# Dummy matmuls only behind the first list, K's first parts from ScalarE's queue, VE's copies on GpSimd, a shorter first list, more slack for the routing

## The chip, the cores and the metric

The kernel runs on one core of a Trainium2 chip. That core has TensorE (PE, matrix products), VectorE (DVE), ScalarE (ACT), GpSimd (POOL) and SyncE (SP), and 16 DMA engines that move data between the device's memory and the core. DMAs are issued from queues of SP, ACT and POOL. The metric is the device time in microseconds (us); the lower, the better.

## The reference

Two stages follow each other: windowed attention over 8 batches of 8 heads, 576 positions and 64 dimensions, and a layer of 8 experts over the 4608 resulting tokens.

```python
scores = scale * np.matmul(q, k.transpose(0, 1, 3, 2))      # [8, 8, 576, 576]
mask = (rel >= 0) & (rel < 64)                              # each row sees 64 positions
attn = softmax(np.where(mask, scores, -1e9))                # over the last axis, + 1e-9
x = np.matmul(attn, v) -> [4608, 512]                       # heads side by side

logits = x @ w_gate                                         # [4608, 8]
for idx in np.argsort(-logits.flatten()):                   # best pair first
    tok, e = idx // 8, idx % 8
    if assigned[tok] >= 0 or counts[e] >= 576: continue
    assigned[tok] = e; counts[e] += 1
for e in range(8):
    mask = assigned == e
    out[mask] = np.maximum(x[mask] @ w1[e], 0) @ w2[e]      # 512 -> 1024 -> 512
```

Each expert so ends with exactly 576 tokens, and which ones is known only when all gates are known and a round of counting is done for the experts in turn.

## The kernel before, in words

**Attention** (`attention`) goes in 72 steps, each for two blocks of 64 positions and four of the eight heads. A step is a short pipeline over PE, DVE and ACT: QK products into a PSUM tile Sp (L126), masked softmax on DVE (L135), exponentials on ACT (L145), transposes on PE (L152), products with the values into Op (L173), and the normalisation into x (L198), which DVE does four steps later. Q, K, VT (the values transposed, for the gates) and VO (the values as they are, with the gate columns beside them) come per batch through SP's queue; batches 0 and 1 come in parts, batch 2 and those behind it whole, and load_all(b) is issued in step 9(b-2)+5. The two loads of K's first part stand on GpSimd's queue. VO has three buffers, VE two. VE is VO shifted by 64 rows, so that windows of the other parity find their rows on the same partitions: `even` makes it by two copies for each tile of positions (L111, L112), on DVE for some tiles and on GpSimd for others. Ahead of `even` the gates of a batch go through PE (gate_mm, L85), ACT (gate_cp), PE (gate_tr, L95) and DVE (gate_out, L101), which writes them into VO.

At the end of attention, when fewer than four steps are in flight, each step also issues five matmuls on a tile of zeros (L274), whose result nobody reads: dummies.

**Routing** (`Routing.steps(p)`) makes expert p's list. Eight rounds narrow down the threshold of the expert whose turn it is: compare on DVE, count by 36 products on PE (L523 for p = 0, L537 for p above), pr on DVE (L569), a product num (L572), a new threshold. Then the list follows: code, eid, q and the marks X on DVE (L616 to L630), a scan, positions by PE (L647, L648), a one-hot product (L687) and the indices idx (L696, L701). The update of eid and of the counts (L708 to L729, with the product cn at L724) is made behind idx. For the first list nothing else is there to do, and the list stands on the path. `warm(n)` issues n dummies (L473); it is called four times a round, after pos, behind the list with 28, and in `turn`.

**Experts** (`Experts`) take three streams each. `load` brings weights: a part `st` by DMA, wh on ACT (L800, fp32 rounded down), -wh into wl on ACT (L809), and an accumulating DMA from GpSimd (L811) that adds st to wl, the low part. Parts 0 to 2 of expert 0 make wl on DVE instead. `turn` gathers the tokens with five indirect DMAs on GpSimd (L853), transposes them on PE (L865), and evacuates them as xh on ACT (L842) and xl on DVE (L845), for five tiles of 128 tokens (the last of 64). `steps` makes the products: 12 matmuls in three groups, wh xh, wl xh, wh xl, into h (L909), hh on ACT (L883) and hl on DVE (L888); then the second products (L941 for the last 64 tokens, L951 for the others), and out through ACT (L923, L926) and an indirect DMA (L931).

**What sets the order.** Attention's order is written out by hand. Behind it a planner, `Streams`, runs routing, loads, turns and products as generators, each yielding an estimate of the time until its next step (`slack` is added to some of these, by SLACK[p]) or a condition; the order in which it takes them is the order of instructions on each engine. A change of one estimate so moves instructions on every engine. The products of expert p start when its XT is set, each unit when its weights stand in W and `tiles` covers its columns.

## Time and profile before

| | us |
|---|---|
| median of 3 runs | 678.64 |
| lowest and highest | 677.87, 678.86 |
| the profiled execution | 681.14 |
| its span in the trace | 679.50 |
| outside the span | 1.64 |
| PE busy | 651.4 (96%) |
| DVE busy | 451.8 (66%) |
| ACT busy | 360.9 (53%) |
| POOL busy | 177.5 (26%) |

The profile is of one execution. The first row of its second part gives PE's busy share in 40 slices of 17 us: it is 9 nearly everywhere, 6 and 8 in the first two, and 8 and 7 in slices 11 and 12, where attention has ended and the first list is made. The row below it on the clock has 6 and 7 there. Busy matmuls are counted whether they are of use or dummies, and a busy PE at a lower clock gets less done, so the busy share must be read with the granted clock (1.00 is 2.4 GHz, 0.50 is 1.2 GHz).

### The profile page before, as it was taken

Reading aid. Unit: us, or ns where it says so; the run is one execution under the profiler, and the core shown is the slowest. Engines: PE = TensorE matmul, PEld = TensorE weight load, DVE = VectorE, ACT = ScalarE, POOL = GpSimd, SP = SyncE. Lnnn points to the kernel's source line nnn. Section 1 sums busy time; section 2 is a strip of 40 time slices with the busy share of each in tenths; the row PEclk is TensorE's granted clock in tenths of the full one; section 3 lists DMA queues with packets and bytes.
Section 4 is the critical chain, followed back from the end, with each engine's and each line's share of the span. In section 5 each row is a group of like instructions: output and inputs, shape, how many; then the busy total and the mean of one; then the engine's idle time right before and its main releaser. Section 6 shows DMA issues by size and latency. Waiting matters only on the chain. (4 is left out here: it accounts for less than half of the span.)

```text
span 679.5 us, 17084 instructions
## 1 busy us (share of the span) xinstructions
PE 651.4 (96%) x6451; PEld 544.1 (80%) x6451; DVE 451.8 (66%) x2262; ACT 360.9 (53%) x733; POOL 177.5 (26%) x203
## 2 busy tenths in 40 slices
PE   6899999999879989999999999999999999999995
PEld 5577777777559868897898799789889889989984
DVE  4989999988677766896896787787777611320300
ACT  4678888886034517617447166355616715634410
POOL 1321222220032116206125133322412443112011
PEclk9899999999679989999999999999999999999998
DMA  8999988922046539849779767939938994952501
GB/s 280 329 357 364 363 309 306 389 96 79 17 143 187 114 75 314 198 80 306 191 143 288 191 147 249 224 82 267 219 101 169 295 273 103 252 150 77 95 23 47
DMA packets 49683, 134.11 MB, mean 197 GB/s; under 512 B 4672, under 2 KB 10432, under 8 KB 49600
## 3 DMA queue, kind: packets, MB, share of 16 engines
q0 software_dynamic: 15552, 54.01, 35.3%
q1 hardware_dynamic: 34048, 79.00, 32.9%
q8 instruction: 51, 0.84, 0.5%
q14 instruction: 32, 0.26, 0.1%
HBM read 82.13 MB, written 18.87 MB: 149 GB/s over the span
## 5 line engine op out<-in xcount | busy, mean ns | idle before, releaser
L888 DVE SCALAR_TENSOR_TENSOR hl<-h,hh 128x256 fp32r<-128x256 f32 x128 | 53.5, 418 | 95.2 <-ACT hh L883 94.5
L951 PE MATMUL o<-wh,hl 128*128 128x512 f32 x256 | 102.1, 399 | 0.0
L951 PE MATMUL o<-wh,hh 128*128 128x512 f32 x256 | 102.1, 399 | 0.0
L951 PE MATMUL o<-wl,hh 128*128 128x512 f32 x256 | 101.3, 396 | 0.0
L145 ACT ACTIVATE pe<-st,mx 128x128 f32<-128x128 f32 x288 | 91.3, 391 | 8.6 <-DVE mx L135 7.2
L883 ACT ACTIVATE hh<-h 128x256 fp32r<-128x256 f32 (+1 forms) x128 | 52.1, 407 | 79.0 <-PE h L909 77.6
L909 PE MATMUL h<-xh,wh 128*128 128x256 f32 (+1 forms) x512 | 93.8, 301 | 0.0
L909 PE MATMUL h<-xh,wl 128*128 128x256 f32 (+1 forms) x512 | 92.0, 298 | 0.0
L909 PE MATMUL h<-xl,wh 128*128 128x256 f32 (+1 forms) x512 | 92.0, 298 | 0.0
L135 DVE CUSTOM_DVE_ANT_0 st<-Sp,mask 128x128 f32<-128x128 f32 x288 | 78.6, 277 | 17.9 <-PE Sp L126 13.4
L931 POOL DMA_INDIRECT out<-ot,idx x40 | 40.2, 1005 | 190.6 <-ACT ot L923 61.6
L923 ACT ACTIVATE ot<-o 128x512 f32<-128x512 f32 x32 | 19.1, 597 | 120.0 <-PE o L951 120.0
L909 PEld LDWEIGHTS h<-xh,wh 128*128 128x128 f32 x512 | 76.6, 190 | 1.4 <-issue 0.7
L909 PEld LDWEIGHTS h<-xh,wl 128*128 128x128 f32 x512 | 75.8, 190 | 0.3
L909 PEld LDWEIGHTS h<-xl,wh 128*128 128x128 f32 x512 | 75.8, 190 | 0.1
L811 POOL DMA_DIRECT2D wl<-st x61 | 55.1, 1065 | 74.7 <-ACT wl L809 58.7
L800 ACT ACTIVATE wh<-st 128x1024 fp32r<-128x1024 f32 x64 | 67.3, 1052 | 12.4 <-DMA st<-w 12.3
L853 POOL DMA_INDIRECT xg<-xs,idx x40 | 42.2, 1054 | 114.9 <-DVE eq L708 62.0
L809 ACT ACTIVATE wl<-wh 128x1024 fp32r<-128x1024 f32 x61 | 64.4, 1056 | 0.4
L951 PEld LDWEIGHTS o<-wl,hh 128*128 128x128 f32 x256 | 48.4, 189 | 9.2
L951 PEld LDWEIGHTS o<-wh,hl 128*128 128x128 f32 x256 | 48.3, 189 | 9.2
L951 PEld LDWEIGHTS o<-wh,hh 128*128 128x128 f32 x256 | 48.4, 189 | 8.9
(177 smaller groups left out, 1164.4 us busy)
## 6 DMA issues: line engine op xcount, KB each, us to landing
wl<-st POOLq DMA_DIRECT2D x61, 512.0 KB, 7.1
st<-w SPq DMA_DIRECT2D x59, 512.0 KB, 7.3
xs<-x SPq DMA_DIRECT2D x36, 256.0 KB, 4.9
VO<-v SPq DMA_DIRECT2D x6, 1168.0 KB, 16.8
VT<-vt SPq DMA_DIRECT2D x6, 1152.0 KB, 11.4
Q<-q SPq DMA_DIRECT2D x6, 1152.0 KB, 13.9
K<-k SPq DMA_DIRECT2D x6, 1152.0 KB, 15.4
st<-w POOLq DMA_DIRECT2D x5, 512.0 KB, 6.0
```

What stands on the lines that cost most here:

```text
L135: nc.vector.tensor_tensor_reduce(st[:, h, :], Sp[h % 2][:, h // 2], mk, scale=-0.125, scalar=3.0e38, op0=OP.add, op1=OP.min, accum_out=mx[ ...
L145: nc.scalar.activation(pe[:, h, :], st[:, h, :], AF.Exp, bias=mx[:, h:h + 1], scale=-1.0)
L800: nc.scalar.activation(hi, st[i], AF.Copy)
L809: nc.scalar.activation(lo, hi.bitcast(FT), AF.Copy, scale=-1.0)
L811: nc.gpsimd.dma_start(lo.bitcast(FT), st[i], accum_op=OP.add)
L853: nc.gpsimd.indirect_dma_start(out=g[0:n, a], out_offset=None, in_=self.xs, in_offset=IndirectOffsetOnAxis(ap=idx[0:n, a:a + 1], axis=0))
L883: nc.scalar.activation(hh[:, f, c0:c1], h, AF.Relu)
L888: nc.vector.scalar_tensor_tensor(t, h[:, a - c0:b - c0], 0.0, hh[:, f, a:b].bitcast(FT), op0=OP.max, op1=OP.subtract)
L909: nc.tensor.matmul(h, wv[:, cc, 128 * (f % 2):128 * (f % 2) + 128], xt[:, cc, c0:c1], start=(k == 0), stop=(k == 11))
L923: nc.scalar.activation(ot, o, AF.Copy)
L931: nc.gpsimd.indirect_dma_start(out=self.out, out_offset=IndirectOffsetOnAxis(ap=idx[0:m, a:a + 1], axis=0), in_=ot[0:m], in_offset=None)
L951: nc.tensor.matmul(o, ht[:, f, 128 * a:128 * a + 128], wt[:, 512 * (f % 2):512 * (f % 2) + 512], start=(k == 0), stop=(k == 23))
```

## The change

K's two loads of the first part of batch 0 are issued from ACT's queue instead of POOL's. `even` runs on DVE for batch 0's first two tiles alone, and on GpSimd for all others; eight pairs of copies move. The dummies of attention's last steps, those of the rounds, the ten after pos and the second six in the first turn go away; 28 behind the list and six in the turn stay. For the first list the operation on eid moves behind idx, and X is made from q directly. XT is set at the start of a turn; a unit of products waits for `tiles`, which counts xh alone, and its third group for `lows`, which counts xl. SLACK is 100 for all experts but the first, and the product cn of experts 2 and up has 1500 ahead of it.

```diff
--- before.py
+++ after.py
@@ -208,8 +208,8 @@
             if b or i[0]:
                 load_qk(b, *i)
             else:
-                load_qk(b, *i, slice(0, 2), nc.gpsimd)
-                load_qk(b, *i, slice(2, 4), nc.gpsimd)
+                load_qk(b, *i, slice(0, 2), nc.scalar)
+                load_qk(b, *i, slice(2, 4), nc.scalar)
                 nc.sync.dma_start(wgbd, wg)
                 counters()
             load_vt(b, *i)
@@ -236,7 +236,7 @@
             put(s + 1, gate_out, b, *i)
             for j in range(4):
                 if i[0] <= 2 * j + 2 < i[1]:
-                    put(s + 1, even, b, j, nc.vector if 4 * b + j <= 2 or (b, j) == (1, 0) or b > 1 and not j else nc.gpsimd)
+                    put(s + 1, even, b, j, nc.gpsimd if b or j > 1 else nc.vector)
     for b in range(2, B):
         put(9 * (b - 2) + 5, load_all, b)
     last = []
@@ -268,11 +268,6 @@
             pv(*seq[s - 3])
         for f, a in at.get(s, []):
             f(*a)
-        if s >= n:
-
-            for _ in range(5):
-                nc.tensor.matmul(SP[0][0].rearrange("p h w -> p (h w)"), z, z[:, None, :].to_broadcast([128, 2, 128]),
-                                 start=True, stop=True)
         if late:
             late.pop(0)()
         if s > 3:
@@ -346,7 +341,7 @@
 NR = 8
 FAR = 2.0 ** 101
 OWN = 2
-SLACK = (0, 0, 0, 0, 100, 100, 100, 100)
+SLACK = (0,) + (100,) * 7
 U32 = mybir.dt.uint32
 
 
@@ -570,8 +565,6 @@
                     yield self.dve(220) + slack
                     num = self.room(128, E, not p)
                     nc.tensor.matmul(num, self.ones[0:ND], pr, start=True, stop=True)
-                    if not p:
-                        self.warm(4)
                     yield self.busy(110) + 200 + slack
                 thr2 = tile_([128, ND], I32, name="thr")
                 if r == 0:
@@ -617,17 +610,20 @@
                                            accum_out=code)
 
             eid = self.eid
-            ab = tile_([128, NJ], FT, name="ab") if p else eid
-            nc.vector.scalar_tensor_tensor(ab, m, T[:, 0:1], best, op0=OP.is_gt, op1=OP.mult)
             self.expert(p, code)
-            yield self.dve(600)
             q = tile_([128, NJ], FT, name="q")
             nc.vector.tensor_scalar(q, best, code, None, op0=OP.is_equal)
+
+            nc.vector.scalar_tensor_tensor(X[:, 1], m, T[:, 0:1], q, op0=OP.is_equal, op1=OP.mult)
+            yield self.dve(600)
             if p:
+                ab = tile_([128, NJ], FT, name="ab")
+                nc.vector.scalar_tensor_tensor(ab, m, T[:, 0:1], best, op0=OP.is_gt, op1=OP.mult)
                 nc.vector.tensor_tensor(eid, eid, ab, OP.add)
-
-            nc.vector.scalar_tensor_tensor(X[:, 1], m, T[:, 0:1], q, op0=OP.is_equal, op1=OP.mult)
-            nc.vector.tensor_scalar(X[:, 0], eid, code, None, op0=OP.is_equal)
+                nc.vector.tensor_scalar(X[:, 0], eid, code, None, op0=OP.is_equal)
+            else:
+
+                nc.vector.scalar_tensor_tensor(X[:, 0], m, T[:, 0:1], q, op0=OP.is_gt, op1=OP.mult)
             yield self.dve(600)
         else:
             pr8 = tile_([128, E], FT, name="pr8")
@@ -646,8 +642,6 @@
         pos = self.room(128, 2 * NJ, not p)
         nc.tensor.matmul(pos, self.tri, Xf, start=True, stop=False)
         nc.tensor.matmul(pos, self.ones, run, start=False, stop=True)
-        if p == 0:
-            self.warm(10)
         yield self.busy(150) + 200 + slack
         Y = tile_([128, 2, NJ], FT, name="Y")
         nc.vector.scalar_tensor_tensor(Y.rearrange("p k j -> p (k j)"), pos, 1.0, Xf,
@@ -704,6 +698,8 @@
         if p < E - 1:
             if p == 0:
                 yield 3000
+            if not p:
+                nc.vector.scalar_tensor_tensor(self.eid, m, T[:, 0:1], best, op0=OP.is_gt, op1=OP.mult)
             eq = tile_([128, NJ], FT, name="eq")
             nc.vector.scalar_tensor_tensor(eq, Y[:, 1], CAP + 0.5, X[:, 1], op0=OP.is_lt, op1=OP.mult)
             nc.vector.scalar_tensor_tensor(self.eid, eq, code[:, 0:1], self.eid, op0=OP.mult, op1=OP.add)
@@ -719,7 +715,7 @@
             c2 = tile_([128, E], BF, name="c2")
             with nc.allow_low_precision(reason="whole numbers up to 36"):
                 nc.vector.tensor_reduce(c2, self.oh.rearrange("p j e -> p e j"), axis=AX.X, op=OP.add)
-            yield self.dve(900) + slack
+            yield self.dve(900) + (slack if p < OWN else 1500)
             cn = self.room(128, E)
             nc.tensor.matmul(cn, self.ones, c2, start=True, stop=True)
             yield self.busy(110) + 200 + slack
@@ -764,6 +760,7 @@
         self.sent = 0
         self.turned = 0
         self.tiles = [0] * E
+        self.lows = [0] * E
 
     def room(self):
         return self.ps.tile([128, 320], FT, name="h", bufs=3)
@@ -840,12 +837,11 @@
             r = slice(128 * a, 128 * a + n)
             t = t.bitcast(FT)
             nc.scalar.activation(xh[:, :, r], t[:, :, :n], AF.Copy)
+            self.tiles[p] = a + 1
             yield 700
             self.busy(600, "dve")
             nc.vector.tensor_tensor(xl[:, :, r], t[:, :, :n], xh[:, :, r].bitcast(FT), OP.subtract)
-            self.tiles[p] = a + 1
-            if a == 1:
-                self.XT[p] = (xh, xl)
+            self.lows[p] = a + 1
 
         g = fw.tile([128, 5, DM], FT, name="xg")
         for a in range(5):
@@ -857,6 +853,7 @@
         yield lambda: self.first == p
         xh = fw.tile([128, NX, CAP], FR, name="xh")
         xl = fw.tile([128, NX, CAP], FR, name="xl")
+        self.XT[p] = (xh, xl)
         for a in range(5):
             n = 128 if a < 4 else 64
             yield max(0, there - 1280 * (4 - a) - self.clock())
@@ -865,7 +862,7 @@
                 nc.tensor.transpose(t[:, cc, :n], g[0:n, a, 128 * cc:128 * cc + 128].bitcast(FR), self.c["identr"][0:n, 0:n])
             dt = self.busy(300)
             self.spawn(evac(a, n, t), dt + 150)
-            if p == 0 and a < 2:
+            if p == 0 and a < 1:
                 self.warm(6)
             yield dt + (1000 if p else 600)
         yield 1500
@@ -904,6 +901,8 @@
             h = self.room()[:, 0:c1 - c0]
             k = 0
             for wt, xt in ((wh, xh), (wl, xh), (wh, xl)):
+                if xt is xl:
+                    yield lambda: self.lows[p] * 128 >= c1
                 wv = wt.rearrange("p (c f) -> p c f", c=NX)
                 for cc in range(NX):
                     nc.tensor.matmul(h, wv[:, cc, 128 * (f % 2):128 * (f % 2) + 128], xt[:, cc, c0:c1],
```

What the planner makes of it at three places follows. PE, from the first expert's second transposes to its first twelve products; before (rps of L473 are dummies, tp the transposes, h the products; only the last of six dummies is shown):

```order
L473 MATMUL rps_4298<-r32_551,ones_331 128x288
L724 LDWEIGHTS ones_331
L724 MATMUL rps_4306<-c2_4290,ones_331 128x8
L909 MATMUL h_4315<-xh_4249,wh_4251 128x256 x3
L865 MATMUL tp_4319<-identr_141,xg_4243 128x128 x4
L909 MATMUL h_4315<-xh_4249,wh_4251 128x256
L909 MATMUL h_4315<-xh_4249,wl_4252 128x256 x4
L909 MATMUL h_4315<-xl_4250,wh_4251 128x256 x4
```

And PE at the same place after, from the last of the six dummies that stay:

```order
L468 MATMUL rps_4212<-r32_551,ones_331 128x288
L862 MATMUL tp_4224<-identr_141,xg_4171 128x128 x4
L908 MATMUL h_4230<-xh_4177,wh_4179 128x256 x3
L720 LDWEIGHTS ones_331
L720 MATMUL rps_4234<-c2_4221,ones_331 128x8
L908 MATMUL h_4230<-xh_4177,wh_4179 128x256
L908 MATMUL h_4230<-xh_4177,wl_4180 128x256 x2
L862 MATMUL tp_4244<-identr_141,xg_4171 128x128 x4
```

The dummies and the count ahead of the first products are gone, and the count (now L720) stands behind three products.

ACT, the conversions of expert 0's last two weight parts (wh and wl) among the evacuations of its products (hh) before:

```order
L883 ACTIVATE hh_4313<-h_4612 128x320
L800 ACTIVATE wh_4666<-st_4415 128x1024
L883 ACTIVATE hh_4313<-h_4641 128x256
L809 ACTIVATE wl_4667<-wh_4666 128x1024
L883 ACTIVATE hh_4313<-h_4678 128x320
L883 ACTIVATE hh_4313<-h_4708 128x256
L800 ACTIVATE wh_4758<-st_4509 128x1024
L883 ACTIVATE hh_4313<-h_4739 128x320
L809 ACTIVATE wl_4759<-wh_4758 128x1024
```

And ACT there after:

```order
L880 ACTIVATE hh_4182<-h_4515 128x320
L880 ACTIVATE hh_4182<-h_4550 128x256
L797 ACTIVATE wh_4584<-st_4342 128x1024
L806 ACTIVATE wl_4585<-wh_4584 128x1024
L880 ACTIVATE hh_4182<-h_4579 128x320
L880 ACTIVATE hh_4182<-h_4613 128x256
L880 ACTIVATE hh_4182<-h_4637 128x320
L797 ACTIVATE wh_4677<-st_4437 128x1024
L806 ACTIVATE wl_4678<-wh_4677 128x1024
```

Each wh now stands behind one more evacuation, directly ahead of its wl.

ACT at the start of expert 1, where its tokens' tiles (xh) come between the last outputs of expert 0 (ot), before:

```order
L923 ACTIVATE ot_5040<-o_4942 128x512
L800 ACTIVATE wh_5055<-st_4930 128x1024
L809 ACTIVATE wl_5056<-wh_5055 128x1024
L800 ACTIVATE wh_5080<-st_4932 128x1024
L809 ACTIVATE wl_5081<-wh_5080 128x1024
L800 ACTIVATE wh_5103<-st_5048 128x1024
L507 COPY one4_5106<-one_75 128x384 x3
L923 ACTIVATE ot_5112<-o_5038 128x512
```

And after:

```order
L502 COPY one4_5044<-one_75 128x384 x3
L806 ACTIVATE wl_5041<-wh_5040 128x1024
L839 ACTIVATE xh_4968<-tp_5056 128x4x128
L922 ACTIVATE ot_5092<-o_5013 128x512
L839 ACTIVATE xh_4968<-tp_5076 128x4x128
L797 ACTIVATE wh_5114<-st_5011 128x1024
L839 ACTIVATE xh_4968<-tp_5103 128x4x128
```

Expert 0's last output to be evacuated but the tail (ot) now stands between expert 1's first and second tile; before, four tiles stood in a row ahead of it.

## Rows read from the trace of the kernel before

**Rows 1.** Windows of two stretches: us, busy by engine, granted clock, DMA share, GB/s.

```profile
20.00:40.00 20.00, 17.16 (x283) 12.16 (x276) 17.83 (x108) 13.34 (x39) 5.75 (x6) 0.91 1.06 353
...
180.00:190.00 10.00, 8.29 (x129) 5.38 (x129) 6.90 (x39) 0.00 (x0) 0.00 (x0) 0.50 0.01 2
```

**Rows 2.** Waits of PE in 0 to 165 us: in total, times, longest.

```profile
PE Sp L126 <- DMA K<-k: 4.2, 2, 3.3
PE Op L173 <- DVE x L198: 2.1, 2, 1.7
```

**Rows 3.** DMA issues in 0 to 40 us: KB each, median us to landing.

```profile
VO<-v SPq DMA_DIRECT2D x1, 1168.0 KB, 18.1
...
Q<-q SPq DMA_DIRECT2D x2, 256.0 KB, 3.1
K<-k POOLq DMA_DIRECT2D x2, 256.0 KB, 6.8
```

**Rows 4.** Windows, the start of the loads.

```profile
4.00:6.00 2.00, 0.52 (x5) 0.25 (x3) 0.23 (x1) 0.00 (x0) 0.00 (x0) 1.00 0.75 152
8.00:10.00 2.00, 1.10 (x20) 0.70 (x24) 0.93 (x8) 0.62 (x3) 0.00 (x0) 1.00 1.05 374
```

**Rows 5.** Timeline of SP's queue: start, us, engine, line, operation, waits.

```profile
30.54 4.10 SPq L72 DMA_DIRECT2D VO<-v  x1
```

**Rows 6.** Timeline of DVE behind the landing of batch 2's VO.

```profile
48.69 0.29 DVE L101 COPY VO<-pvt 128x128 f32<-128x128 f32 x1
49.08 0.95 DVE L111 COPY VE<-VO 64x584 f32<-64x584 f32 x1
50.04 0.46 DVE L112 COPY VE<-VO 64x584 f32<-64x584 f32 x1
```

**Rows 7.** Timeline, dummies (PE) and the rounds (DVE).

```profile
164.03 0.72 PE L274 MATMUL Sp<-zero 128*128 128x256 bf16 x5
...
172.48 0.15 DVE L569 TENSOR_SCALAR pr<-rps 15x8 bf16<-15x8 f32 x1 [0.38 <-PE rps L523]
174.80 0.15 DVE L569 TENSOR_SCALAR pr<-rps 15x8 bf16<-15x8 f32 x1 [0.31 <-PE rps L523]
177.38 0.15 DVE L569 TENSOR_SCALAR pr<-rps 15x8 bf16<-15x8 f32 x1 [0.57 <-PE rps L523]
...
177.68 1.14 PE L473 MATMUL rps<-r,ones 128*128 128x288 bf16 x4
```

**Rows 8.** Timeline, the first list's end and expert 0's first products.

```profile
188.72 0.25 DVE L621 SCALAR_TENSOR_TENSOR eid<-m,base,best 128x36 f32<-128x36 f32 x1
...
194.66 3.60 PE L473 MATMUL rps<-r,ones 128*128 128x288 bf16 x28
...
200.35 0.53 PE L865 MATMUL tp<-identr,xg 128*128 128x128 f32 x4 [2.09 <-DMA xg<-xs,idx]
...
202.67 0.60 ACT L842 ACTIVATE xh<-tp 128x512 fp32r<-128x512 f32 x1 [1.16 <-PE tp L865]
...
204.18 0.78 PE L909 MATMUL h<-xh,wh 128*128 128x256 f32 x3
```

**Rows 9.** Timeline and a window, the last weights of expert 0.

```profile
234.03 1.05 ACT L800 ACTIVATE wh<-st 128x1024 fp32r<-128x1024 f32 x1
...
242.02 0.73 PE L941 MATMUL o<-wl,hh 128*128 128x512 f32 x1 [0.38 <-DMA wl<-st]
...
242.00:246.00 4.00, 3.98 (x11) 2.75 (x12) 2.15 (x9) 0.59 (x1) 0.50 (x1) 0.57 0.01 4
```

**Rows 10.** Waits of PE in 250 to 660 us.

```profile
PE rps L724 <- DVE c L721: 1.5, 1, 1.5
PE rps L537 <- DVE G L466: 1.2, 2, 1.1
```

**Rows 11.** Timeline of POOL: gathers of expert 0's and of expert 1's tokens.

```profile
195.87 2.11 POOL L853 DMA_INDIRECT xg<-xs,idx  x1 [42.15 <-ACT wh L800]
...
257.93 1.00 POOL L853 DMA_INDIRECT xg<-xs,idx  x1 [4.83 <-DVE eq L708]
```

## The prediction, made before the changed kernel had run

> **What bounds the kernel now.** I read the table by stages first, then the waits of TensorE (PE), then the landings of the loads, and only then single instructions. The profiled execution took 681.14 us (span 679.50, 1.64 around it); the median of the runs is 678.64, 2.50 lower. The sum is made on the profiled one and carried over as a difference.
>
> The expert phase is bound by PE and nearly free of waits: behind 250 us its two largest waits are 1.5 and 1.2 us [rows 10]. What the change can touch lies ahead of that. In 20 to 40 us PE is busy 17.16 of 20 us at a mean granted clock of 0.91, between its two levels of 1.2 and 2.4 GHz, while the DMA engines are full, with a share of 1.06 [rows 1]. PE's first waits of attention are for K, 4.2 us, the longer one 3.3, and then 2.1 for the normalised values x [rows 2]. In 180 to 190 us, the search for the first list, PE looks busy, 8.29 of 10, yet most of that is dummies, DVE 6.90, and the granted clock is 0.50, the low level [rows 1].
>
> One load decides how much of an early gain survives: VO of batch 2 (the values and their gates). It is issued at 30.54 [rows 5] and lands 18.1 later [rows 3], at 48.64; VectorE's (DVE's) first copy into that tile, L101, starts at 48.69 [rows 6]. So DVE waits there for the stream of loads and not for its own work, and what PE does behind it waits too.
>
> **The change part by part.**
>
> *K from ScalarE's queue.* K's two loads from GpSimd's queue take 6.8 us to land, Q's equal loads from SyncE's 3.1 [rows 3]; PE waits 3.3 for K [rows 2]. First products can so come 0 to 3.3 us earlier. What counts is whether the stream gets ahead. In 4 to 6 us it moves 152 GB/s, in 8 to 10 it moves 374 [rows 4]: filling the first would bring all later loads 2.0 x (1 - 152/374) = 1.2 us forward. Bounds 0 (K lands as before) and 2.0 (the whole stretch); I take 1.2, since the stream is full from then on to 40 us [rows 1]. The two issues stand at the head of ScalarE, ahead of its table load; what is queued behind is the first exponential, which needs products and a softmax first: nothing. GpSimd's constants start earlier by as much as two issues.
> The first-byte latency in the Trainium skill, "DMA: Bandwidth & Descriptors", Specifications, is about 1 us from GpSimd and about 0.6 from ScalarE; by it K would gain only 0.4 and the time would come to 674.2. The landings differ by 3.7 [rows 3], so I don't go by it.
>
> *VE's copies on GpSimd.* Eight pairs leave DVE. At the limiting place two of them, 0.95 and 0.46 us, stand right behind L101 [rows 6], ahead of the next softmax: 1.4 us. GpSimd is busy 5.75 of 20 us there [rows 1], so that it takes them beside; if it were late, products of odd tiles would wait for VE. Should the cover be gone, the cost is about one copy, 0.95. Moving them also ends PE's wait for x, if it is these copies that delay x: 0 to 1.7 [rows 2].
> So attention's end comes 1.2 + 1.4 = 2.6 earlier by the landing. PE alone would be faster by more, 1.2 + 1.7 + the clock given back in 20 to 40 us, 20 x 0.09 = 1.8: 4.7. The 2.1 between them become a wait at the landing, after which the clock is low for a while: in 20 to 40 us, waits of about 3 us went with 1.8 lost, so 0 to 1.4; I take 0.8. **Attention: -1.8** (0 to -4.7).
>
> *Dummies and the first list.* Five dummies at 164.03 take 0.72 and stand ahead of transposes that attention's end waits for [rows 7]; 0.5 of that is on the path. The fifteen others stand where PE waits for DVE: nothing. In each of eight rounds DVE's L569 waits for the counting products. From 172.48 to 174.80 is 2.32; from 174.80 to 177.38 it is 2.58, its wait 0.57 and not 0.31, since four dummies (1.14 at the low clock) stand ahead of the counts [rows 7]. Five of the seven steps are the long ones: 5 x 0.26 = 1.3. If the counts were slow by the clock instead, nothing; if the dummies delay all seven by one of theirs, 7 x 1.14/4 = 2.0. The list loses one DVE step, 0.25, overlapped in part [rows 8]: 0.15. **-1.95** (-0.5 to -2.7).
>
> *Start of the products.* Behind the list 28 dummies run 3.60 from 194.66, are over before the first gather lands, and the transposes start at 200.35, still on the gather [rows 8]. The first product starts at 204.18, behind the second six dummies and a count; the second token tile, which is all it needs in after, is there at 202.67 + 0.60 = 203.27 [rows 8]. That is 0.91, of which I count nine tenths: **-0.8** (0, if the tile itself comes later, to -1.6, if the six dummies that stay, 6 x 3.60/28 = 0.77, cost nothing any more).
>
> *Last weights of expert 0.* Where PE ends expert 0's first half it waits for these, 0.38 at 242.02 [rows 9]. In after the conversion L800 of the last two parts stands one evacuation later on ScalarE, and the last is directly ahead of L809, not overlapped with the wait for the products: one L800, 1.05 [rows 9], later at GpSimd and so at PE: **+1.1** (0 to 2).
>
> *Expert 1's start.* Its list is routed with more slack, so its last transposes come behind expert 0's last product, and the first product waits for a conversion that stands behind L923 on ScalarE. Such a conversion takes 0.60 [rows 8]; with a little for its semaphore **+0.65** (0.3 to 2: all three, if more of them pile up).
>
> *More slack.* The count L724 waits 1.5 once and L537's products 1.2 [rows 10]; both go behind more products. L724's whole wait and three quarters of L537's: **-2.4** (-1.2 to -2.7). Elsewhere the later lists still come ahead of the products they feed: nothing.
>
> The sum: -1.8 - 1.95 - 0.8 + 1.1 + 0.65 - 2.4 = -5.2. The profiled run would take 675.9, the median 678.64 - 5.2 = **673.4**. Its own range is 671.5 to 675.5: one of the terms at its far bound, attention aside, moves it by 1 to 1.4, two of them by some 2.
>
> **The rivals.**
>
> *The landing does not limit.* If VO of batch 2 comes earlier by all of PE's gain (its buffer or issue moves up too), attention gives 4.7 and not 1.8: 673.4 - 2.9 = **670.5**. For it: every load's issue hangs on work that gets faster. Against: the stream is full from 20 to 40 us [rows 1].
>
> *The clock stays low.* Without dummies PE does little through the list. The 28 behind it then run at the low level, 3.60 x 2 = 7.2 [rows 8], and end at 201.9, 1.5 behind the place at which the transposes could start; and products after that run low for a while, as in 242 to 246, mean 0.57 behind a wait [rows 9], 4 x 0.43 = 1.7. Price 3.2: **676.6**. For it: the clock is at the low level wherever PE has little to do. Against: with dummies it is 0.50 in 180 to 190 as well [rows 1], so that they bought nothing there, and the 28 stay.
> The Trainium skill, "TensorE: Matmul & The Clock Gate", What's actually happening, says that the default state is throttled and that activity releases it; this speaks against taking dummies out, and this rival is its result. The rows agree for the 28 behind the list, 3.60 us, and not for the rounds.
>
> *The waits only move.* K lands no earlier from the other queue or a landing later than this one keeps its place, so attention gives 0; and the waits of the late routing turn up at its next step. 673.4 + 1.8 + 2.4 = **677.6**, no change. For it: the stream is full, and a step that is given slack takes that time from the next list. Against: the later lists have room.
>
> *Expert 1's weights late: slower.* On GpSimd five gathers stand ahead of the transfers that finish expert 1's first weights. They took 1.00 each; for the first list one took 2.11 [rows 11]. If the later list puts them where other transfers run, at 2.11 each, the weights come 5 x 1.11 = 5.55 late; I count 0.5 of room, and a low clock behind the wait, 1.7 [rows 9]: +6.8, **680.2**. It decides where a gather takes more than 1.00 + 0.5/5 = 1.1. For it: lists and weights come closer together in after. Against: expert 1's own row has 1.00.
>
> **How the numbers follow.** The forecast has 0.52, the landing that doesn't limit 0.12, the low clock 0.12, waits that only move 0.13, late weights 0.11. About 0.2% is what a measurement can tell from no change: 677.3 to 680.0. So faster has 0.52 + 0.12 + 0.12 = 0.76, no change 0.13, slower 0.11. The range takes in the forecast's own 671.5 to 675.5, the low clock, most of "only move" and the upper half of the first rival: 669.8 to 677.8.
>
> **What the profile of after would show.** K's landing from ScalarE at 3 to 4 us, the wait for K about 1 us or none. DVE's L101 of batch 2 still directly behind the landing, near 47.4, with PE's wait of about 2 us there; the first transposes behind attention 1.8 + 0.5 = 2.3 earlier. Steps of 2.32 between the L569 of the rounds, at the low clock; a step still at 2.58 would show that the dummies weren't the cause. The first product within 0.2 us of the end of the second token tile's conversion. A wait for `wl` of about 1.5 at the end of expert 0's first products, one of 0.65 at expert 1's first. No wait of L724 over 0.3. The prediction is wrong if K's landing stays near 6 us, if the 28 dummies take 7 us, or if expert 1's first products wait for weights.

## The result, and the profile after

The changed kernel took 683.07 us (median of 6 runs, 680.94 to 684.52), the one before 678.75 beside it (677.63 to 680.23): a ratio of 1.006, 95% interval 1.0036 to 1.0083. It is **slower by about 4 us**, where the forecast had 673.4 and faster.

One thing has to be known for the reading: the execution of the changed kernel that was profiled took 680.94, the shortest of its six, and that of before took 681.14, longer than each of its six runs here. The two spans, 679.3 and 679.5, are equal by that chance. So the traces show where time was won and lost, and less than all of the loss. Times of kernels from different comparisons are not exactly like for like either: the median of before beside them went from 678.7 to 680.2.

| start of | before | after | after against before |
|---|---|---|---|
| first transposes of tokens (PE) | 200.35 | 195.83 | -4.5 |
| expert 0's first product | 204.18 | 198.09 | -6.1 |
| expert 1's first product | 271.21 | 266.11 | -5.1 |
| expert 2's first product | 332.69 | 331.96 | -0.7 |
| expert 7's first product | 621.10 | 621.15 | 0.0 |

Up to the first product the change won 6.1 against this trace, where the sum had 4.6. The trace of before was a late one, however: four other kernels of the experiments, with attention and dummies as before, have expert 0's first product at 202.16 to 202.75, and against them it is 4.1 to 4.7. Between expert 1's first product and expert 2's the change lost 4.4. The waits of PE in 0 to 165 us, the answer to [rows 2] (in total, times, longest), and the windows at the landing of batch 2's VO (us, busy by engine, granted clock, DMA share, GB/s):

```profile
PE Sp L126 <- DMA K<-k: 1.4, 2, 0.8
...
PE Op L173 <- DVE x L198: 0.3, 1, 0.3
```

```profile
44.00:48.00 4.00, 3.47 (x64) 2.16 (x62) 1.96 (x12) 2.45 (x8) 1.18 (x2) 1.00 1.03 330
48.00:52.00 4.00, 3.65 (x64) 2.72 (x59) 3.92 (x34) 3.29 (x11) 1.80 (x4) 1.00 1.06 393
```

And DVE there, the answer to [rows 6]; first the instruction that stands right ahead of L101 in the trace of before, then L101 after:

```profile
48.24 0.42 DVE L198 TENSOR_TENSOR x<-Op,r 128x256 f32<-128x256 f32 x1
```

```profile
46.43 0.29 DVE L101 COPY VO<-pvt 128x128 f32<-128x128 f32 x1 [2.00 <-DMA VO<-v]
```

After, the landing ends a wait of 2.00 of DVE's, 2.26 us earlier than 48.69. Before there was no such wait: L198 ended at 48.66 and L101 followed at 48.69, with the landing at 48.64. The prediction read a wait for the loads into that row, but DVE's own queue was as late as the load. PE is short of work at the landing after, 3.47 and 3.65 of 4 us, but keeps the full clock.

From 250 us on the waits of PE are these, the answer to [rows 10]:

```profile
PE rps L532 <- DVE G L461: 4.7, 3, 3.8
PE h L908 <- ACT xh L839: 0.6, 1, 0.6
```

L724's wait of 1.5 is gone, as forecast. In its place there is one of 3.8 us at expert 1, with a lower clock behind it (0.59 on average in 280 to 284). PE's timeline (start, us, engine, line, tiles, count, idle before) and a window:

```profile
266.11 0.62 PE L908 MATMUL h<-xh,wh 128*128 128x256 f32 x3 [0.61 <-ACT xh L839]
...
275.13 0.75 PE L908 MATMUL h<-xl,wh 128*128 128x320 f32 x4
279.69 0.59 PE L532 MATMUL rps<-G,one 128*128 128x60 bf16 x9 [3.81 <-DVE G L461]
280.11 0.93 PE L908 MATMUL h<-xh,wh 128*128 128x320 f32 x4
280.84 1.27 PE L908 MATMUL h<-xh,wl 128*128 128x320 f32 x4
```

```profile
280.00:284.00 4.00, 4.00 (x22) 4.00 (x21) 1.70 (x9) 3.09 (x5) 0.87 (x1) 0.59 1.07 211
```

Four products of 320 columns took 0.75 before the wait and 1.27 behind it. What PE waits for is G, the input of a count for the next list, which is not urgent; but that count stands in PE's order ahead of more of expert 1's products. The chain can be followed back through the engines. DVE first, then ACT, then SP's queue:

```profile
273.46 0.21 DVE L554 STREAM_TRANSPOSE pt<-pq 128x32 f32<-128x32 f32 x1
277.92 0.42 DVE L885 SCALAR_TENSOR_TENSOR hl<-h,hh 128x256 fp32r<-128x256 f32 x1 [4.25 <-ACT hh L880]
278.26 0.16 DVE L557 TENSOR_REDUCE ps<-pt 128x1 f32<-128x15 f32 x1
...
276.56 1.06 ACT L797 ACTIVATE wh<-st 128x1024 fp32r<-128x1024 f32 x1 [4.75 <-DMA st<-w]
277.52 0.37 ACT L880 ACTIVATE hh<-h 128x256 fp32r<-128x256 f32 x1
...
266.69 0.33 SPq L780 DMA_DIRECT2D st<-w  x1
```

DVE's next step for the list (L557) stands behind hl, the low part of a product's result, which waits 4.25 for hh, the high part. On ACT hh stands behind the conversion of a weight part, which waits 4.75 for its fetch. And that fetch left SP only at 266.69. SP's waits say why, and POOL's timeline what came ahead:

```profile
SPq L780 <- DMA wl<-st: 16.9, 2, 14.6
```

```profile
255.50 1.01 POOL L849 DMA_INDIRECT xg<-xs,idx  x1 [1.74 <-DVE eq L704]
...
260.86 0.92 POOL L849 DMA_INDIRECT xg<-xs,idx  x1 [0.30 <-issue]
261.77 1.97 POOL L808 DMA_DIRECT2D wl<-st  x2
```

It is the fetch of expert 1's seventh part. There are six buffers `st`, so it needs that of the first part, which is free when the accumulating DMA that reads it (L808) has landed; and that DMA stands on POOL behind the five gathers of expert 1's tokens. The part itself belongs to the second products, which start at 301.49, more than 20 us later. What makes it dear is that ACT's order puts its conversion ahead of an evacuation.

### The profile page after: what moved, and what is told of

Its sections match the earlier page's. It is cut to its first block, busy times and chain, and to the rows that moved or that the text cites. A ratio compares the mean times of both kernels' runs of the same rounds, so it can differ in the third digit from the quotient of the medians.

```text
span 679.3 us, 16951 instructions
## 1 busy us (share of the span) xinstructions
PE 640.0 (94%) x6383; PEld 537.4 (79%) x6383; DVE 444.7 (65%) x2246; ACT 362.6 (53%) x733; POOL 184.2 (27%) x217
## 5 line engine op out<-in xcount | busy, mean ns | idle before, releaser
L135 DVE CUSTOM_DVE_ANT_0 st<-Sp,mask 128x128 f32<-128x128 f32 x288 | 78.7, 277 | 21.8 <-PE Sp L126 14.1
L808 POOL DMA_DIRECT2D wl<-st x61 | 56.4, 1176 | 58.8 <-ACT wl L806 50.7
L849 POOL DMA_INDIRECT xg<-xs,idx x40 | 40.0, 1000 | 63.2 <-DMA st<-w 40.3
```

The lines of the kernel that those rows point to most:

```text
L135: nc.vector.tensor_tensor_reduce(st[:, h, :], Sp[h % 2][:, h // 2], mk, scale=-0.125, scalar=3.0e38, op0=OP.add, op1=OP.min, accum_out=mx[ ...
L808: nc.gpsimd.dma_start(lo.bitcast(FT), st[i], accum_op=OP.add)
L849: nc.gpsimd.indirect_dma_start(out=g[0:n, a], out_offset=None, in_=self.xs, in_offset=IndirectOffsetOnAxis(ap=idx[0:n, a:a + 1], axis=0))
```

## The experiments

Two theories at first. **Order**: the planner's edits (slack, above all) put expert 1's list and weights later against PE's products. **Stream**: the DMA engines are full from 250 to 280 us in any case, and an early gain ends there.

**The early edits alone** (K's queue, VE's copies, the dummies; before's planner order):

```diff
-                load_qk(b, *i, slice(0, 2), nc.gpsimd)
-                load_qk(b, *i, slice(2, 4), nc.gpsimd)
+                load_qk(b, *i, slice(0, 2), nc.scalar)
+                load_qk(b, *i, slice(2, 4), nc.scalar)
...
+                    put(s + 1, even, b, j, nc.gpsimd if b or j > 1 else nc.vector)
...
-            for _ in range(5):
...
-                        self.warm(4)
...
-            self.warm(10)
...
-            if p == 0 and a < 2:
+            if p == 0 and a < 1:
```

> The kernel before with only the edits that leave the planner's order alone: K's two loads on ScalarE's queue, VE's copies on GpSimd, the dummies gone that the change removes. Theory order (the loss comes from the planner's edits, which put the list and the weights of expert 1 later against PE's products): all of the 5 to 6 us gained up to the first product stay, 672.5 to 674. Rival stream (the DMA engines are full from 250 to 280 us whatever the order, and an early gain ends there in a wait for weights): 677 to 680, with a wait of ScalarE for st of 3 us or more behind expert 1's start.

676.60 against 679.42, ratio 0.995 (0.9929 to 0.9971): some 3 us are kept. That lies between the times of the two theories. **The slack alone**, and **the change with the old slack**:

```diff
-SLACK = (0, 0, 0, 0, 100, 100, 100, 100)
+SLACK = (0,) + (100,) * 7
```

> The kernel before with only SLACK = 0, then 100 for all other experts. Theory order: slower than before by 4 to 6, 682 to 685, the time lost in the first half of expert 1's products. Rival stream: within 1 of before, since the stretch is as full as before.

> The changed kernel with SLACK as it was before (0 for experts 0 to 3). Theory order: the loss of about 4.6 in expert 1's first half goes and the early gain stays, 674 to 677. Rival stream: 682 to 684, as with the slack.

The slack on the kernel before: 686.82, ratio 1.010 (1.0072 to 1.0128), 7.4 us slower, more than the 4 to 6 expected. The change without it: 675.76, ratio 0.9937 (0.9914 to 0.9959), 7.3 below the changed kernel (from another comparison; by the ratios to before it is 8.3). So one constant carries more than the whole loss, and the theory of the order has its place right. On the slack's own trace ACT's wait for the seventh part is 5.42, and what stands behind it is a token tile:

```profile
279.28 1.06 ACT L800 ACTIVATE wh<-st 128x1024 fp32r<-128x1024 f32 x1 [5.42 <-DMA st<-w]
280.24 0.37 ACT L842 ACTIVATE xh<-tp 128x256 fp32r<-128x256 f32 x1
...
280.66 1.43 PE L909 MATMUL h<-xh,wh 128*128 128x320 f32 x4 [4.40 <-ACT xh L842]
```

With the old slack in the changed kernel the same wait is

```profile
276.53 1.06 ACT L797 ACTIVATE wh<-st 128x1024 fp32r<-128x1024 f32 x1 [0.90 <-DMA st<-w]
```

The fetch leaves SP at the same time as in the changed kernel (266.86 and 266.69), but expert 1's first product is at 269.76 and not at 266.11: the fetch is 2.9 us ahead of that product and not 0.6 behind it.

**The planner's edits alone** (the changed kernel with K, VE and dummies as before):

> The changed kernel with K's loads back on GpSimd's queue, VE's copies where they were and all dummies back: the planner's edits alone. Theory order: 686 to 690, the early gain missing on top of the loss. Rival stream: 682 to 684, since the early gain was lost at expert 1's weights anyway.

688.11, ratio 1.0115 (1.0085 to 1.0144). The early edits give 5.0 on top of the planner's ones (688.11 to 683.07; by the ratios 3.7). So they are not lost in this stretch; the theory of the stream wanted 682 to 684 here.

**The mechanism in two ways.** Seven buffers, with every engine's order unchanged; and the conversion of the seventh part moved behind two more evacuations, with the fetches unchanged:

```diff
-STAGE = 6
+STAGE = 7
```

> The changed kernel with seven buffers for weight parts in place of six; every engine's order stays the same. Theory buffer (expert 1's seventh fetch waits for the buffer of the first part, which is freed by an accumulating DMA behind five gathers on GpSimd; ScalarE then waits for that fetch ahead of an evacuation that PE's counts and products need): the fetch leaves some 10 us earlier, the wait of 3.8 for G and the low clock behind it go, 676 to 679. Rival bandwidth (the DMA engines are full there, so the part lands when it did, or takes from the gathers): 682 to 684.

```diff
-                (LOAD if p else 1500 if i < 3 else 4000) * (1 if i else 2)
+                (LOAD if p else 1500 if i < 3 else 4000) * (1 if i else 2) + 6000 * (p == 1 and i == 6)
```

> The changed kernel with the planner told that expert 1's seventh weight part comes 6 us later, which moves its conversion behind two more evacuations on ScalarE; the fetches stay. Theory buffer: the part still lands late, but no evacuation stands behind it, and the loss goes: 676 to 679. Rival bandwidth, or a wait of PE for the weights themselves: 682 or more, since the parts behind it come later still.

678.87 (ratio to before 0.9983, 0.9962 to 1.0004) and 678.02 (0.9969, 0.9948 to 0.999): 4.2 and 5.0 below the changed kernel (other comparisons; by the ratios 5.2 and 6.2). With seven buffers SP waits for one fetch, the eighth, the seventh leaves at 253.14, and PE's wait for G falls from 3.8 to 0.5; with the later conversion the part still comes late, but PE goes on:

```profile
SPq L780 <- DMA wl<-st: 15.5, 1, 15.5
...
PE rps L532 <- DVE G L461: 0.5, 1, 0.5
```

```profile
276.20 0.44 ACT L880 ACTIVATE hh<-h 128x320 fp32r<-128x320 f32 x1 [1.38 <-PE h L908]
278.60 1.06 ACT L797 ACTIVATE wh<-st 128x1024 fp32r<-128x1024 f32 x1 [1.96 <-DMA st<-w]
```

(The first fence is of the kernel with seven buffers, SP's waits in 245 to 290 and PE's in 250 to 300 us; the second of the kernel with the later conversion.) Either end of the chain breaks it: the buffer, or the place of the conversion.

The rest of the slack's 7.3, some 3 us, stays with seven buffers. That trace has two short waits at expert 1's start and a low clock behind them:

```profile
267.27 0.62 PE L908 MATMUL h<-xh,wh 128*128 128x256 f32 x3 [0.61 <-ACT xh L839]
269.11 0.84 PE L908 MATMUL h<-xh,wl 128*128 128x256 f32 x4 [0.73 <-DMA wl<-st]
```

```profile
268.00:272.00 4.00, 3.27 (x20) 3.08 (x19) 2.86 (x14) 2.79 (x6) 0.06 (x1) 0.70 1.05 234
272.00:276.00 4.00, 4.00 (x37) 3.76 (x36) 2.16 (x8) 3.14 (x5) 2.62 (x3) 0.87 1.04 222
```

1.3 of waits and 4 x 0.30 + 4 x 0.13 = 1.7 of clock come to 3.0. That these are the rest is not shown: it is read from one trace and was not tried by itself.

**The parts of the early edits.** K's queue alone, and VE's copies alone (the lines of the first diff above):

> The kernel before with K's two loads on ScalarE's queue alone. If the landing of batch 2's VO sets attention's pace, its end comes 2.2 earlier, as that landing does in the changed kernel, and not by the 2.8 that the first product gains: 676 to 678 if it is kept to the end. If the landing does not set it: 2.9 earlier or 0.

> The kernel before with only VE's copies moved to GpSimd. If the landing sets the pace, attention ends 1.4 earlier, the two copies behind L101, and not by the 1.7 that PE waits for x at 29 us: 677 to 679. If GpSimd's copies come late: 0, or slower by one copy, 0.95.

679.86, ratio 0.9983 (0.996 to 1.0006), and 680.70, ratio 1.0005 (0.9979 to 1.003): neither can be told from no change. DVE's L101 of batch 2 with K alone, with VE alone, and with both:

```profile
47.40 0.29 DVE L101 COPY VO<-pvt 128x128 f32<-128x128 f32 x1
```

```profile
48.89 0.29 DVE L101 COPY VO<-pvt 128x128 f32<-128x128 f32 x1 [3.29 <-DMA VO<-v]
```

```profile
46.65 0.29 DVE L101 COPY VO<-pvt 128x128 f32<-128x128 f32 x1 [2.38 <-DMA VO<-v]
```

With K alone L101 follows DVE's own work, with VE's copies in it, without a wait, as it did before: 47.40 is 1.3 earlier than 48.69, of the 2.2 by which the landing moved. With VE alone DVE is early and waits 3.29 for a landing that is where it was. The two limits stood together; only both edits move the step by 2. What VE's copies free behind L101 is lost again when they move alone, for PE waits too and its clock falls:

```profile
49.24 0.75 PE L85 MATMUL pvt<-VT,wgs 128*32 128x320 f32 x8 [1.82 <-DVE VO L101]
```

```profile
52.00:56.00 4.00, 4.00 (x65) 3.03 (x65) 2.90 (x23) 2.10 (x8) 1.92 (x3) 0.72 1.06 394
```

Attention's last products start at 165.64 with K alone and at 166.78 with VE alone, against 166.94 before.

**K and VE together, dummies as before**, **the dummies alone**, **seven buffers alone**, and **the dummies with seven buffers**:

> K's queue and VE's copies together, dummies as before. If both are needed (the landing gives 2.2, the copies behind it 1.4): attention ends 3.5 earlier and the time is 676 to 678. If they add nothing to each other, as each alone measured: 679 to 680.

> The kernel before with only the dummies gone that the change removes (20 in attention's last steps, 32 in the rounds, 10 behind the positions, the second six in the first turn). Theory of the prediction: 0.5 + 1.3 and, since the trace with the early edits alone shows the first product 2.35 behind the first transposes and not 3.83, 1.5 at the start of the products: 3.3 earlier there, 675 to 677.5 if it is kept. Rival clock (TensorE stays at the low level and the 28 dummies end late): 679 to 682.

> The kernel before with seven buffers for weight parts, nothing else. If the buffer costs only where the list comes late (theory buffer as it stands), before gains 0 to 1: 679 to 680. If it holds expert 1's weights in before as well, and the early edits run into it, 677 to 678 or less.

> The removed dummies alone, with seven buffers. If the 2.7 that they gain up to the first product are lost at the buffer, they are kept here: 2.5 to 3 below the run with seven buffers alone. If they are lost to the clock or to the later waits, the same as that run.

Together K and VE give 676.46, ratio 0.9965 (0.9946 to 0.9985), and attention's last products start at 163.35. The dummies alone: 681.41, ratio 1.002 (0.9995 to 1.0044). Seven buffers alone: 679.32, ratio 0.9999 (0.9979 to 1.002). Dummies and buffers: 677.94, ratio 0.9998 (0.9976 to 1.002). So the dummies cost nothing that can be measured at the end, and the seventh buffer brings nothing measurable where nothing is early.

**The early edits with seven buffers**, the change with the old slack and seven buffers, the 1500 ahead of the later counts alone, and the early edits with both:

```diff
-            yield self.dve(900) + slack
+            yield self.dve(900) + (slack if p < OWN else 1500)
```

> The kernel before with the early edits alone (K's queue, VE's copies, the dummies) and seven buffers for weight parts. Theory buffer: ScalarE's wait of 2.8 for expert 1's seventh part goes, and with it PE's wait of 1.8 for G: 674 to 675.5. If that wait is free: 676 to 677, as with the early edits alone.

> The changed kernel with SLACK as before and seven buffers for weight parts. Theory buffer: with the list early enough the fetch is hardly late (its wait was 0.9), so that the seventh buffer brings at most 1: 674.5 to 676. Rival (a whole different delay was taken away with the slack): 671 to 673.

> The kernel before with only the 1500 ahead of the counts for experts 2 and up. Theory of the prediction: PE's wait of 1.5 for that count goes and the time with it, 677 to 678.5. Rival move (the later experts' products end when their weights and lists allow, or the list's other steps wait in its place): within 0.5 of before.

> The early edits, seven buffers and the 1500 ahead of the later counts, the slack and the order of the list as before. If what each gave adds up (front with seven buffers 6.0, the counts 1.9): 672 to 673. If the counts' wait only moves: 674 to 675.

| kernel | us | ratio to before | 95% interval |
|---|---|---|---|
| early edits, seven buffers | 674.23 | 0.9915 | 0.9888 to 0.9941 |
| change, old slack, seven buffers | 674.83 | 0.9925 | 0.9901 to 0.9949 |
| before, 1500 for the counts | 678.32 | 0.9975 | 0.9957 to 0.9994 |
| early edits, seven buffers, 1500 | 673.26 | 0.9925 | 0.99 to 0.995 |

With a seventh buffer the early edits give 6.0 us and not 2.8 (by the ratios 5.8 and 3.4, and the two intervals overlap a little). So without it a part of the lead probably ended at the same buffer even with the old slack. The traces bear it out: PE's longest wait for G is 1.8 with the early edits alone and 0.2 with the buffer, and this is ACT's wait for the seventh part, without and with it:

```profile
273.42 1.06 ACT L791 ACTIVATE wh<-st 128x1024 fp32r<-128x1024 f32 x1 [2.83 <-DMA st<-w]
```

```profile
273.13 1.06 ACT L791 ACTIVATE wh<-st 128x1024 fp32r<-128x1024 f32 x1 [0.60 <-DMA st<-w]
```

In the expectation for the old slack with seven buffers I had at most 1 to win; 0.9 it was (675.76 to 674.83, two comparisons). The counts' 1500 gave 1.9 alone, and on the early edits nothing sure (ratios 0.9915 and 0.9925). The versions with early edits and seven buffers beat the kernel before by 0.75 to 0.85%, and so the changed one by more.

## Why the prediction was wrong

The forecast was faster, 673.4 with a range to 677.8; it came out slower, 683.07.

*The place was seen, its price was not.* The failing step is **More slack, -2.4**; its loss falls at the place that **Expert 1's start, +0.65** speaks of. I read the slack as time for two late counts and looked for harm in PE's order at one boundary. The wait named there came as forecast, 0.61 at 266.11. What I didn't follow is what a later list moves on the other queues: gathers ahead of accumulating DMAs on POOL, buffers behind those, a fetch on SP behind the buffer, a conversion on ACT behind the fetch, and an evacuation behind that. Each link could be read from the trace of before: there the seventh fetch left 2.0 us ahead of expert 1's first product (269.20 and 271.21), in the changed kernel 0.6 behind it, with the slack alone 1.3 behind it. ACT's wait for it is 0.64, 4.75 and 5.42 in these three. The slack measured +7.4 (on the kernel before) and +7.3 (in the change). In the sum the step had -2.4, of which the count's own 1500 accounts for the 1.5 of L724; the slack's part, -0.9, has the wrong sign. Of the +7.3 the chain at the buffer is 4.2 to 5.0; where the other 2 to 3 arise is not shown.

*The slower rival* had the queue right, five gathers ahead of the accumulating DMAs on GpSimd, and the wrong reason. The gathers take 1.0 on average, as before (one took 1.22), and PE doesn't wait for weights at expert 1; it was enough that they stood closer to the products. Its condition, gathers above 1.1, would have ruled it out, and its chance of 0.11 was too low for a chain with so little room.

*Attention, -1.8*: the size was too small, and one premise was wrong. K landed 4.5 us behind its issue and not 6.8, and the stream of loads came 2.2 forward and not 1.2 [rows 4], a little beyond the bound of 2.0. From L101 to the next masked softmax (L135) it is 1.06 after and 2.22 before, so the copies gave 1.2 of their 1.4 [rows 6]. The low clock that I charged 0.8 for did not come, 1.00 in both windows at the landing; with VE alone it did, 0.85 and 0.72 in 48 to 56. Attention's last products start 3.6 earlier with K and VE together (163.35 for 166.94), and 2.8 to 3.3 earlier than in the four other traces with attention as before. The premise: DVE did not wait for the landing before, its own queue was as late; none of the seven traces with K and VE as before has a wait for it there. So each edit alone gave little, which was in none of the steps; I took the landing for the only limit. In the changed kernel DVE does wait for it, 2.00, which speaks against the first rival, though that rival's 4.7 for attention was nearer.

*Dummies and list, -1.95*: five steps of 2.58 became 2.32, as forecast (`warm` is called once in each round, for four dummies):

```profile
170.39 0.15 DVE L564 TENSOR_SCALAR pr<-rps 15x8 bf16<-15x8 f32 x1 [0.32 <-PE rps L518]
172.71 0.15 DVE L564 TENSOR_SCALAR pr<-rps 15x8 bf16<-15x8 f32 x1 [0.31 <-PE rps L518]
```

From attention's last products to the list's indices it is 27.85 before and 26.53 after, 1.3 less, and the shorter list gave none of its 0.15. The 0.5 for attention's five dummies isn't shown: with the dummies alone attention's last products start at 166.56, within the 166.13 to 166.94 of the traces with attention as before. *Start of the products, -0.8*: wrong by its base. From the indices to the first product it is 9.39 in the trace of before, 9.03 after; but it runs from 7.92 to 9.50 in the seven other traces with all dummies, and from 8.25 to 9.27 in the nine other ones without. So the execution that I read was a late one, and the step gave nothing. Its clock shows why. A window of before behind its 28 dummies (3.60 [rows 8]), and the 28 dummies of the kernel with seven buffers alone, which has all dummies too:

```profile
202.00:204.00 2.00, 2.00 (x10) 1.36 (x11) 1.16 (x2) 0.60 (x1) 1.70 (x2) 0.50 0.65 166
```

```profile
194.10 5.79 PE L473 MATMUL rps<-r,ones 128*128 128x288 bf16 x28
```

In before, and with K alone, the clock had risen when the 28 dummies began; they took 3.60, PE then waited 2.1 to 2.2 for the gather, and the clock was low again, 0.50, shortly ahead of the first product. In the six other traces with all dummies the 28 took 5.10 to 5.79, and the first product came 7.92 to 9.04 behind the indices. That the early steps together came near the forecast 4.6 is luck: attention gave more, the list less, the start of the products nothing. Why the 1.3 of the rounds doesn't show at the end with the dummies alone (ratios 1.002 and, with seven buffers, 0.9998 like the buffers alone) stays open.

*The clock rival.* The 28 dummies took 5.07 after and 3.60 before, which looks like what this rival said. But with all dummies they took 5.10 to 5.79 in six of eight traces, so the dummies that went away are not the cause. In the changed kernel the transposes still waited for the gather behind them:

```profile
188.93 5.07 PE L468 MATMUL rps<-r,ones 128*128 128x288 bf16 x28
195.83 0.53 PE L862 MATMUL tp<-identr,xg 128*128 128x128 f32 x4 [1.84 <-DMA xg<-xs,idx]
196.21 0.91 PE L468 MATMUL rps<-r,ones 128*128 128x288 bf16 x6
```

They ended 1.8 ahead of the landing, and the six dummies after it run at 0.15 each. The rule of the Trainium skill, "TensorE: Matmul & The Clock Gate", What's actually happening, is that the default is throttled and activity releases it. The changed kernel agrees, with 0.50 in 184 to 188, where PE is busy 1.22 of 4 us, and 1.00 in 192 to 194, behind the start of the 28; the rounds of before don't, with 0.50 in 184 to 188 at 3.42 of 4. Nor is the clock low wherever PE has little to do, as the rival had it: in 4 to 6 us it is 1.00 with PE busy 0.52 of 2 [rows 4]. The low clock cost nothing at the list in the changed kernel; it did behind PE's wait of 3.8 at expert 1.

*Last weights, +1.1*: in the trace the waits for them are 1.1 in all at 0.8 and 0.3, against 0.4 before, and expert 0's second half, to expert 1's first product, took 37.06 and not 35.59. That half takes 35.16 to 37.90 in the six kernels with the planner's edits (with the new slack or the old), and 34.08 to 36.89 in the twelve others. The sign and the size fit, but no run tells apart how much of it is the conversion's place. *Expert 1's start*: the wait was 0.61, as forecast.

*Late waits*: the 1.5 was worth having, 1.9 for the counts alone; the rest of that step was the slack's loss.

## What to carry to other kernels

A planner's constant that delays one stream moves every queue that the stream shares: before it is changed, write down for the first stage behind it what each in-order queue then has ahead of what, down to the buffers that those transfers free. A wait for data that is needed much later still stalls everything behind it in the queue, so either give the load a buffer of its own or put the step that uses it later. And where two limits end at nearly the same time, as a landing at 48.64 and an engine's own queue at 48.66 do here, relieving one gives little: test them together. A row without a wait in it doesn't show which of the two held the step.

## What the runs showed that I had not expected

Executions of one kernel differ by 3 us and more here, and the traces show one reason. A short wait of PE sometimes costs its length alone and sometimes a stretch at the low clock on top. This is the same place, behind expert 0's first products, with K alone and with VE alone; PE is idle there for 2.0 and for 2.4 of eight us:

```profile
236.00:240.00 4.00, 2.44 (x26) 1.72 (x25) 2.43 (x11) 0.00 (x1) 0.86 (x1) 1.00 0.61 116
240.00:244.00 4.00, 3.60 (x15) 2.50 (x15) 2.81 (x12) 0.59 (x1) 0.51 (x1) 1.00 0.11 19
```

```profile
236.00:240.00 4.00, 2.60 (x19) 1.65 (x18) 2.81 (x15) 0.57 (x1) 0.85 (x1) 1.00 0.49 94
240.00:244.00 4.00, 2.99 (x16) 1.76 (x15) 1.12 (x6) 0.54 (x1) 0.00 (x0) 0.75 0.22 43
244.00:248.00 4.00, 4.00 (x21) 3.01 (x22) 2.33 (x9) 0.05 (x1) 0.98 (x1) 0.83 0.15 33
```

The first keeps the clock at 1.00, the second falls to 0.75 and 0.83, and expert 0's second products take 34.12 in the one and 36.09 in the other. Such a wait has to be priced both ways, and a forecast of under 1% for this kernel needs more than one execution of before.
